# The gather of an mLSTM stage in matmuls of 32 stationary columns, at a higher priority

## The chip, the cores and the metric

The kernel runs on one core of a Trainium2 chip. The metric is the device time of one execution in microseconds (us). The time before is the median of three runs, 572.12 us (571.66 to 572.26). Profiles are taken of one execution.

## The reference

An mLSTM runs over 768 tokens for 4 batches of 8 heads with 40 values a head; its output, 3072 tokens of 320 values, goes through a gated feed-forward network of width 1536.

```
for t in range(S):
    m_new = max(f[t] + m, i[t])
    C = exp(f[t] + m - m_new) * C + exp(i[t] - m_new) * outer(v[t], k[t])
    n = exp(f[t] + m - m_new) * n + exp(i[t] - m_new) * k[t]
    y[t] = sigmoid(o[t]) * (C @ q[t]) / max(abs(n @ q[t]), 1)
x = y.transpose(0, 2, 1, 3).reshape(B * S, H * D)
out = (sigmoid(x @ w_gate) * (x @ w_val)) @ w_out
```

## The kernel before

The recurrence is worked out in chunks of 128 tokens. A unit `u = (c, b)` is chunk `c` (0 to 5) of batch `b` (0 to 3), all 8 heads of it: 24 units. Within a unit the contribution of its own tokens is a matrix product: `dm[u]`, 128 source tokens by 8 heads by 128 target tokens, holds decays times scores, and `vt[u]`, 128 tokens by 8 heads by 41, holds the values with a column of ones, which gives the denominator. What came before the chunk is in the state `cst`.

A unit passes through five stages. `st_a` transposes q and k. `st_b` makes the scores on TensorE, in groups of 3, 3 and 2 heads, and multiplies each group into `dm[u]` on VectorE (L427 in chunks 0 and 1, L435 afterwards). `st_c` does the part with the state (`in`, L447, for chunks after the first), then the gather: for each head one f32 matmul with `dm[u][:, h, :]` as the stationary operand, 128 columns, and `vt[u][:, h, :]`, 41 columns, as the moving one, into `pv` in PSUM (`av`, L452). VectorE adds `pv` to the state's part (L454) and the denominator and output gate follow. `st_d` transposes the result (`xt`, L488) and splits it into a high and a low f32r part. `st_e` updates the state (`cs`, L500).

The feed-forward network runs in between, chunk by chunk: `ffn_up` (L532, L534, L537 into `pg`) and `ffn_down` (L554 to L556 into `po`), each product as three f32r products of high and low parts. Its matmuls move 256, 512 or 320 columns. Weights come from DRAM and are decoded and split on the other engines during the first part of the kernel.

The order is set in two ways. The first two units' work, `opening`, is emitted in an order by hand, with its own `gather` (L697). After it all events (stages of units, tiles of the network, weight parts) are sorted by the positions in `PARAM['pos']` and emitted one after another; a scheduler then orders the instructions of each engine by priority, which falls with the order of emission, as far as dependences allow. `tc.high_priority(offset=n)` lifts the instructions in its block by n places; stages a to d are emitted with an offset of `PARAM['HPO']`, 1. TensorE runs its queue in the resulting order.

PSUM tiles of the stages come from `bank`, two buffers of the tag `pa` in turn. The gate transposes of `gate_transpose` (L195) are small matmuls on 32 partitions.

Of the kernel before, what the change touches and what calls it, by code (L numbers as in the profile page):

```python
# [67 lines left out]
    },  # L68
    'unpin': [],
}  # L70
GROUPS = ((0, 3), (3, 3), (6, 2))

# [2 lines left out]
def mlstm_then_gated_ffn_kernel(  # L75
# [13 lines left out]
    nc = tc.nc  # L89
    B, H, S, D = q.shape  # L90
    P = 128
# [30 lines left out]
    qt, kt, vt, ot = {}, {}, {}, {}  # L122
# [18 lines left out]
    dm = {}  # L141

    def dm_tile(c, b):
        dm[(c, b)] = big.tile([P, H, L], F32, tag="dmat", name=f"d_{c}_{b}", bufs=3)
        return dm[(c, b)]
# [193 lines left out]
    def bank(c, b, shape, name):  # L339
        return ps_a.tile(shape, F32, tag="pa", name=f"{name}_{c}_{b}")  # L340
# [51 lines left out]
    def stack():  # L392
# [6 lines left out]
        for x, dst, i in ((1, ks, 0), (0, qs, 1)):  # L399
# [4 lines left out]
            nc.sync.dma_start(dst[one].rearrange("p (m g) t -> p m (g t)", m=3).bitcast(F32),  # L404
                              sc[:, 0, :, x, :].rearrange("m d w -> d m w"))

    dlast = {}

    def d_last(u):
# [29 lines left out]
    def st_c(c, b):  # L439
        u = (c, b)  # L440
        nc.scalar.activation(ot[u], ot[u], AF.Tanh, scale=0.5)
        t1 = None
        if c > 0:
            pi = bank(c, b, [P, H, DA], "in")
            for g, (h0, nh) in enumerate(GROUPS):
                r = nh * D
                nc.tensor.matmul(pi[:, h0 : h0 + nh, :], qk[u][:r, g, :], cst[:r, b, g, : nh * DA], start=True, stop=True)  # L447
            t1 = two.tile([P, H, DA], F32, tag="t1", name=f"t1_{c}_{b}")
            nc.vector.tensor_tensor(t1, pi, dec[:, c, b * H : (b + 1) * H].unsqueeze(2).broadcast_to([P, H, DA]), ALU.mult)
        pv = bank(c, b, [P, H, DA], "av")  # L450
        for h in range(H):
            nc.tensor.matmul(pv[:, h, :], dm[u][:, h, :], vt[u][:, h, :], start=True, stop=True)  # L452
        if c > 0:
            nc.vector.tensor_tensor(t1, t1, pv, ALU.add)  # L454
            hs = t1
        else:
            hs = pv
        halfden(u, hs)
        times_den(u)
# [4 lines left out]
    def halfden(u, hs):  # L464
        c, b = u
        den = two.tile([P, H], F32, tag="den", name=f"den_{c}_{b}")
        nc.vector.tensor_scalar(den, hs[:, :, D], -2.0, 2.0, ALU.mult, ALU.max)
        nc.vector.scalar_tensor_tensor(den, hs[:, :, D], 2.0, den, ALU.mult, ALU.max)
        nc.vector.reciprocal(den, den)
        rden[u] = den  # L470
        nc.vector.scalar_tensor_tensor(ot[u], ot[u], 1.0, hs[:, :, :D], ALU.add, ALU.mult)

    def times_den(u):
        c, b = u
        xin[u] = x = two.tile([P, 3 * P], F32, tag="x", name=f"x_{c}_{b}", bufs=1)
        eng = E('ro0' if c == 0 and b < 2 else 'ro')
        eng.tensor_tensor(x[:, :DM].rearrange("p (h d) -> p h d", d=D), ot[u],
                          rden[u].unsqueeze(2).broadcast_to([P, H, D]), ALU.mult)
        E('xd0' if c == 0 and b < 2 else 'xd').tensor_copy(x[:, DM:], x[:, 2 * P : DM])
# [94 lines left out]
    def opening():  # L574
        us = ((0, 0), (0, 1))
# [48 lines left out]
        d = [dm_tile(0, b) for b in range(2)]  # L624
# [5 lines left out]
        pmb, pt, ps, pv, pc, px, sp = {}, {}, {}, {}, {}, {}, {}  # L630
# [5 lines left out]
        def ptile(tag, shape, name):  # L636
            return (ps_a if tag == "pa" else ps_o).tile(shape, F32, tag=tag, name=name)
# [56 lines left out]
        def gather(b):  # L694
            pv[b] = p = ptile(tags["v", b], [P, H, DA], f"av_0_{b}")
            for h in range(H):
                nc.tensor.matmul(p[:, h, :], d[b][:, h, :], vt[us[b]][:, h, :], start=True, stop=True)  # L697

        def ogate(b):
            nc.scalar.activation(ot[us[b]], ot[us[b]], AF.Tanh, scale=0.5)  # L700
# [7 lines left out]
        w = {x: None for x in ((0, 0), (1, 0), (2, 0))}  # L708
# [25 lines left out]
        for b in range(2):  # L734
            for n in range(2):
                op(f"sp{b}{n}", spread, (b, n))
                op(f"ex{b}{n}", expd, (b, n), f"sp{b}{n}")
                op(f"mk{b}{n}", mask, (b, n), f"ex{b}{n}")
            op(f"dl{b}", d_last, (us[b],), f"mk{b}0", f"mk{b}1")
            for g in range(3):  # L740
                op(f"tr{b}{g}", trans, (b, g))
                op(f"cp{b}{g}", copy, (b, g), f"tr{b}{g}")
                op(f"qb{b}{g}", qbd, (b, g), f"cp{b}{g}")
                op(f"sc{b}{g}", score, (b, g), f"qb{b}{g}")
                op(f"ti{b}{g}", times, (b, g), f"sc{b}{g}", f"dl{b}")
            op(f"kw{b}", kweight, (b,), f"dl{b}", *(f"tr{b}{g}" for g in range(3)))
            op(f"og{b}", ogate, (b,))
            op(f"ga{b}", gather, (b,), *(f"ti{b}{g}" for g in range(3)))
            op(f"na{b}", norm_a, (b,), f"ga{b}", f"og{b}")
            op(f"nb{b}", norm_b, (b,), f"na{b}")  # L750
            op(f"xt{b}", st_d, us[b], f"nb{b}")
# [33 lines left out]
    start = [0.0]  # L785
# [9 lines left out]
    for u in range(2, NU):  # L795
        for st in "abcde":
            c, b = divmod(u, B)
# [16 lines left out]
    for u in reversed(range(2, NU)):  # L814
# [5 lines left out]
        n = u + (1 if u == B * (PARAM['V32'] + 1) - 1 else 2)  # L820
# [19 lines left out]
    for u in range(2, NU):  # L840
        c, b = divmod(u, B)
# [18 lines left out]
    def emit(p, kind, kk):  # L860
# [7 lines left out]
        elif kind == "w":  # L868
            with tc.high_priority(offset=PARAM["WPO"]):
                w_next(wseq[kk])  # L870
        elif kind == "g":
            if kk == 0:
                dmat_load(1, 0)
            else:
                gates_of(2, NCH)
        elif kind == "h":
            gate_transpose(ag, at, *((1, 2), (2, NCH))[kk], None)
        elif kind == "k":
            gates_turn(*((1, 2), (2, NCH))[kk])
        elif kind == "e":  # L880
            if last is None:
                dmat(c, b)
            else:
                with tc.issue_after(last.ins):
                    dmat(c, b)
        else:
            with tc.high_priority(offset=PARAM["HPO"]):
                if kind == "a":
                    st_a(c, b)
                elif kind == "b":  # L890
                    st_b(c, b)
                elif kind == "c":
                    st_c(c, b)
                    st_e(c, b)
                    prefetch(c + 1, b)
                else:
                    st_d(c, b)
# [45 lines left out]
```

## Time and profile before

| | |
|---|---|
| median of three runs | 572.12 us |
| span of the profiled execution | 569.9 us |
| gathers after the opening (L452) | 22 units, 352 matmul records |
| gathers in the opening (L697) | 2 units, 32 matmul records |
| TensorE matmuls and weight loads | 3587 each |
| granted TensorE clock, mean | 0.988 |

The profile names engines PE (TensorE matmuls), PEld (TensorE weight loads), DVE (VectorE), ACT (ScalarE), POOL (GpSimd). A row of a group has the line, the engine, the operation, output and inputs with shapes, the count, then busy us and mean ns of one, then the idle time of the engine ahead of it and what ended it. A record `128*128` is rows by stationary columns; `128x41` is the moving operand. An f32 matmul shows as two records, an f32r one as one. The records of matmuls overlap, so the distance from one start to the next tells more than a duration. The chain of work that ended last is followed back from the end of the kernel, step by step, to what released each piece.

### The profile page before, as it was taken

How to read it: one execution, taken by the hardware profiler on the slowest of the kernel's cores; microseconds unless marked ns; L12 is line 12 of the kernel's file. 1: busy time of each engine (PE TensorE's matmuls, PEld its weight loads, DVE VectorE, ACT ScalarE, POOL GpSimd, SP SyncE). 2: the span in 40 equal slices, each digit the busy share in tenths (PEclk: the TensorE clock that was granted, in tenths of full speed). 3: DMA queues.
4: the chain of work that ended last, by engine and by line, in shares of the span. 5: the costliest groups of instructions: out<-in, count | busy, mean ns of one | idle time of the engine just before them, and what ended most of it. 6: DMA issues, size and time to landing. Idle time of an engine off the chain costs nothing.

```text
span 569.9 us, 9906 instructions
## 1 busy us (share of the span) xinstructions
PE 546.7 (96%) x3587; PEld 497.0 (87%) x3587; DVE 319.5 (56%) x739; ACT 232.2 (41%) x581; POOL 162.2 (28%) x231
## 2 busy tenths in 40 slices
PE   8667999999999999999999999999999999999997
PEld 7565988788899999998888888888888888999996
DVE  5788878895755645555555544545543545432322
ACT  5285657754443442352243241433342332232322
POOL 5567646575420241311322310332210210000000
PEclk9789999999999999999999999999999999999999
DMA  9797747242674947354666544685644824010000
GB/s 197 193 240 185 202 123 192 93 115 54 169 173 119 183 103 182 100 147 125 167 125 156 132 141 129 149 171 124 140 125 134 206 56 121 4 47 2 24 2 23
DMA packets 131641, 72.27 MB, mean 127 GB/s; under 512 B 103113, under 2 KB 120777, under 8 KB 131593
## 3 DMA queue, kind: packets, MB, share of 16 engines
q1 hardware_dynamic: 130504, 71.39, 50.6%
q8 instruction: 28, 0.46, 0.3%
q10 hardware_dynamic: 1088, 0.26, 0.2%
q14 instruction: 21, 0.16, 0.1%
HBM read 56.95 MB, written 14.68 MB: 126 GB/s over the span
## 4 chain that ended last, share of the span: by engine, by line
PE 85%; DVE 7%; ACT 3%; issue 2%; POOL 2%; POOLq 0%; DVEq 0%; ACTq 0%
PE pg L532 34%; PE po L554 7%; PE po L556 7%; PE po L555 7%; PE av L452 6%; PE pg L534 6%; PE pg L537 6%; PE in L447 2%; PE s L434 2%; PE pt L373 2%; PE xt L488 2%; PE cs L500 2%; PE s L426 1%; DVE dc L264 1%; ACT d L226 1%
## 5 line engine op out<-in xcount | busy, mean ns | idle before, releaser
L539 ACT ACTIVATE sg<-pg 128x256 f32<-128x256 f32 (+1 forms) x103 | 48.3, 469 | 174.3 <-PE pg L537 174.2
L540 DVE SCALAR_TENSOR_TENSOR sg<-sg,pg 128x256 f32<-128x256 f32 (+1 forms) x103 | 53.9, 524 | 113.9 <-ACT sg L539 110.6
L532 PE MATMUL pg<-xh,wl 128*128 128x256 f32 (+1 forms) x412 | 111.1, 342 | 1.2 <-POOL wl L304 1.2
L532 PE MATMUL pg<-xh,wh 128*128 128x256 f32 (+1 forms) x412 | 110.9, 343 | 0.4 <-DVE sg L540 0.4
L532 PE MATMUL pg<-xl,wh 128*128 128x256 f32 (+1 forms) x412 | 108.7, 339 | 0.0
L556 PE MATMUL po<-oh,gl 128*128 128x320 f32 x288 | 93.0, 323 | 0.0
L554 PE MATMUL po<-oh,gh 128*128 128x320 f32 x288 | 92.3, 321 | 0.4 <-ACT gh L543 0.4
L555 PE MATMUL po<-ol,gh 128*128 128x320 f32 x288 | 92.4, 321 | 0.0
L544 DVE TENSOR_TENSOR gl<-sg,gh 128x256 fp32r<-128x256 f32 (+1 forms) x103 | 59.6, 579 | 35.5 <-ACT gh L543 34.9
L532 PEld LDWEIGHTS pg<-xh,wl 128*128 128x128 f32 x412 | 70.9, 191 | 8.5 <-POOL wl L304 1.4
L532 PEld LDWEIGHTS pg<-xh,wh 128*128 128x128 f32 x412 | 70.9, 191 | 5.8 <-DVE sg L540 0.6
L532 PEld LDWEIGHTS pg<-xl,wh 128*128 128x128 f32 x412 | 69.3, 190 | 6.6
L543 ACT ACTIVATE gh<-sg 128x256 fp32r<-128x256 f32 (+1 forms) x103 | 51.7, 502 | 47.7 <-DVE sg L540 47.7
L554 PEld LDWEIGHTS po<-oh,gh 128*128 128x128 f32 x288 | 54.5, 189 | 2.0 <-ACT gh L543 0.6
L555 PEld LDWEIGHTS po<-ol,gh 128*128 128x128 f32 x288 | 54.4, 189 | 1.3
L556 PEld LDWEIGHTS po<-oh,gl 128*128 128x128 f32 x288 | 54.2, 188 | 0.5 <-DVE gl L544 0.2
L534 PE MATMUL pg<-xh,w 128*128 128x256 f32 (+1 forms) x206 | 52.9, 332 | 0.7 <-POOL v L139 0.4
L537 PE MATMUL pg<-xl,w 128*128 128x256 f32 (+1 forms) x206 | 53.1, 331 | 0.0
L452 PEld LDWEIGHTS av<-v,d 128*128 128x128 f32 x352 | 46.8, 191 | 2.2 <-DVE d L427 0.6
L452 PE MATMUL av<-v,d 128*128 128x41 f32 x352 | 45.5, 269 | 0.4 <-DVE d L427 0.3
L508 POOL TENSOR_TENSOR cst<-cst,cdec 120x246 f32<-120x246 f32 (+1 forms) x32 | 16.0, 519 | 98.9 <-PE in L447 98.9
L235 POOL TENSOR_SCALAR_AFFINE_SELECT d<-d 128x1024 f32<-128x1024 f32 x22 | 24.2, 1101 | 50.1 <-ACT d L230 46.0
(128 smaller groups left out, 834.5 us busy)
## 6 DMA issues: line engine op xcount, KB each, us to landing
d<-mscr SPq DMA_DIRECT2D x22, 512.0 KB
ks<-scr SPq DMA_DIRECT2D x16, 360.0 KB
qs<-scr SPq DMA_DIRECT2D x16, 360.0 KB
k<-in_k_dram SPq DMA_DIRECT2D x24, 160.0 KB
v<-in_v_dram SPq DMA_DIRECT2D x24, 160.0 KB
o<-in_o_gate_dram SPq DMA_DIRECT2D x24, 160.0 KB
st_o<-in_moe_w_out_dram SPq DMA_DIRECT2D x12, 320.0 KB
out_dram<-ob SPq DMA_DIRECT2D x24, 160.0 KB
```

Of the source, the lines that this page charges most:

```text
L235: nc.gpsimd.affine_select(out=d, in_=d, pattern=[[0, H], [1, L]], compare_op=ALU.is_ge, fill=0.0, base=0, channel_multiplier=-1)
L452: nc.tensor.matmul(pv[:, h, :], dm[u][:, h, :], vt[u][:, h, :], start=True, stop=True)
L532: nc.tensor.matmul(pg[n], w[n][:, a, fs], x[c][:, a, n0:n1], start=(i + a == 0), stop=False)
L534: nc.tensor.matmul(pg[n], w2[n][:, fs], xh[c][:, 2, n0:n1], start=False, stop=False)
L537: nc.tensor.matmul(pg[n], w2[n][:, fs], xl[c][:, 2, n0:n1], start=False, stop=True)
L539: nc.scalar.activation(sg, pg[0], AF.Tanh, scale=0.5)
L540: nc.vector.scalar_tensor_tensor(sg, sg, 1.0, pg[1], ALU.add, ALU.mult)
L543: last = nc.scalar.activation(gh[u][:, :nt], sg, AF.Copy)
L544: E('gl0' if c == 0 else 'gl').tensor_tensor(gl[u][:, :nt], sg, gh[u][:, :nt].bitcast(F32), ALU.subtract)
L554: nc.tensor.matmul(po[t], g1[:, ts], oh[:, j, :], start=(j == 0), stop=False)
L555: nc.tensor.matmul(po[t], g1[:, ts], ol[:, j, :], start=False, stop=False)
L556: nc.tensor.matmul(po[t], g0[:, ts], oh[:, j, :], start=False, stop=(j == NF - 1))
```

## The change

A helper `by_columns` splits one matmul into n matmuls, each with 128/n of the stationary columns (a part of the target tokens) and the whole moving operand, and writes each to the matching partitions of the output. With n = 4 both gathers, in `st_c` and in the opening, issue four matmuls of 32 stationary columns for each head, one quarter of the tokens after another. In `st_c` the gather is emitted with a priority offset of 20 within the block's offset of 1. The entries `SC` and `SPO` of `PARAM` are not used.

```
+    'AV': 4,
+    'SC': 1,
+    'APO': 20,
+    'SPO': 20,
...
+    def by_columns(dst, lhs, rhs, n):
+        w = P // n
+        for x in range(n):
+            xs = slice(x * w, (x + 1) * w)
+            nc.tensor.matmul(dst[xs], lhs[:, xs], rhs, start=True, stop=True)
...
         pv = bank(c, b, [P, H, DA], "av")
-        for h in range(H):
-            nc.tensor.matmul(pv[:, h, :], dm[u][:, h, :], vt[u][:, h, :], start=True, stop=True)
+        with tc.high_priority(offset=PARAM['APO']):
+            for h in range(H):
+                by_columns(pv[:, h, :], dm[u][:, h, :], vt[u][:, h, :], PARAM['AV'])
...
             for h in range(H):
-                nc.tensor.matmul(p[:, h, :], d[b][:, h, :], vt[us[b]][:, h, :], start=True, stop=True)
+                by_columns(p[:, h, :], d[b][:, h, :], vt[us[b]][:, h, :], PARAM['AV'])
```

## Prediction

> **What bounds the kernel now.** I read first the busy line and the chain of the page, then the windows, then the chain in order of time around one gather.
>
> ```profile
> span 569.9 us, 9906 instructions
> PE 546.7 (96%) x3587; PEld 497.0 (87%) x3587; DVE 319.5 (56%) x739; ACT 232.2 (41%) x581; POOL 162.2 (28%) x231
> ...
> PE 85%; DVE 7%; ACT 3%; issue 2%; POOL 2%; POOLq 0%; DVEq 0%; ACTq 0%
> ...
> PE pg L532 34%; PE po L554 7%; PE po L556 7%; PE po L555 7%; PE av L452 6%; PE pg L534 6%; PE pg L537 6%; PE in L447 2%; PE s L434 2%; PE pt L373 2%; PE xt L488 2%; PE cs L500 2%; PE s L426 1%; DVE dc L264 1%; ACT d L226 1%
> ```
>
> TensorE carries 85% of the chain, and the gather (`av`, L452) is 6% of it, some 34 us. The windows say where TensorE is the limit:
>
> ```profile
> core 0: us, PE busy (x) PEld busy (x) DVE busy (x) ACT busy (x) POOL busy (x), PEclk, DMA share, GB/s
> 12.00:30.00 18.00, 12.90 (x68) 10.91 (x68) 13.01 (x27) 7.63 (x22) 10.06 (x15) 0.73 0.81 209
> 60.00:495.00 435.00, 431.28 (x2788) 388.00 (x2786) 250.24 (x582) 176.07 (x427) 127.24 (x171) 1.00 0.54 135
> ```
>
> Between 60 and 495 us matmuls lack only 3.7 of 435 us, and VectorE, the next engine, has 250. What a gather takes there is added to the end or taken from it one for one. Twenty gathers lie in that stretch, two just before it and two in the opening:
>
> ```profile
> L452 PE MATMUL av<-v,d 128*128 128x41 f32 x352 | 45.5, 269 | 0.4 <-DVE d L427 0.3
> ...
> L697 PE MATMUL av<-v,d 128*128 128x41 f32 x32 | 5.3, 338 | 2.2 <-DVE d L689 2.2
> ```
>
> 352 records are 22 units of 16, and 32 are 2: each of 8 heads is two records (an f32 matmul runs as two loads and two matmuls). One unit in the chain, in order of time (start, length, what):
>
> ```profile
> 169.26 0.63 PE in L447 x6
> 169.89 1.75 PE av L452 x16
> 171.65 0.20 PE pg L532
> 171.84 0.57 PE cs L500 x6
> ```
>
> The gather takes 1.75 us, 0.109 a record. What is that? `cs` has 4 records of 120 stationary columns and 2 of 80, 640 columns in 0.57 us, or 0.89 ns each; the gather loads 16 x 128 = 2048 columns, 0.85 ns each. The moving side is far from it (41 columns against up to 123 in `cs`), so the **weight loads** set the pace. For the moving side I take the f32 scores, which move 384 columns, in the chain of the second chunk:
>
> ```profile
> 77.01 0.65 PE s L426 x2
> ```
>
> Two records in 0.65 us, 0.85 ns a column: 41 columns are 35 ns. Today 16 x 35 ns = 0.56 us of movement lie hidden under 1.75 us of loads.
>
> **The change part by part.** *The split.* Each head becomes four matmuls of 32 stationary columns. The columns loaded stay 2048 a unit, as 64 loads of about 32 x 0.87 = 28 ns. The moving operand passes four times: 64 records of 35 ns, 2.24 us if one follows another, against 0.56. So nothing is removed; the change pays only if column groups work beside each other. No row shows that, so I bound it. One after another: 2.24 us. All four groups at once: 16 x 35 ns = 0.56 us. Two at once: 1.12 us. I take two. The reason is the order: the two records of one f32 matmul use the same group and stand next to each other, so the next group's first load can go beside the second load of this one, but the one after that must wait until its own group's first record has started, and matmuls start in order in every row I read. Saved: 1.75 - 1.12 = 0.63 us a unit.
>
> The Trainium skill (TensorEngine Tiling (Array Packing), section Overview) puts the speedup of four groups of 32 columns at up to 4x; by that estimate a gather would be 0.44 us, and no run here shows it.
>
> *The switch.* The only place where TensorE works on a part of its array is the gate transpose L195, on 32 of 128 rows. Matmuls first, then loads:
>
> ```profile
> 93.24 0.47 PE L532 MATMUL pg<-xh,wh 128*128 128x512 f32 x1
> 93.73 0.43 PE L195 MATMUL ptg<-ident,gin 32*128 32x32 f32 x4
> 94.09 0.49 PE L532 MATMUL pg<-xh,wh 128*128 128x512 f32 x1
> ...
> 93.73 0.32 PEld L195 LDWEIGHTS ptg<-ident,gin 32*128 32x128 f32 x4 [0.32 <-DVE qk L359]
> 94.09 0.19 PEld L532 LDWEIGHTS pg<-xh,wh 128*128 128x128 f32 x1
> ...
> L195 PE MATMUL ptg<-ident,gin x11: 221/223/282, 4.7 to 93.9; 32*128 32x32 f32 x11
> ```
>
> Compare a whole-array stretch:
>
> ```profile
> 462.03 0.19 PEld L554 LDWEIGHTS po<-oh,gh 128*128 128x128 f32 x1
> ...
> 462.18 0.31 PE L554 MATMUL po<-oh,gh 128*128 128x320 f32 x1
> 462.33 0.31 PE L452 MATMUL av<-v,d 128*128 128x41 f32 x2
> 462.47 0.40 PE L555 MATMUL po<-ol,gh 128*128 128x320 f32 x1
> 462.70 0.31 PE L452 MATMUL av<-v,d 128*128 128x41 f32 x2
> ```
>
> Normally a load starts some 0.15 us ahead of its matmul. After the 32-row group the next load starts with its matmul, at 94.09. L195's group ends at 93.73 + 0.43 = 94.16 and one of its matmuls takes 0.22 (the median in its row), so the last one started at 93.94 and 0.15 us passed, of which its own 32 columns explain 0.03: 0.12 us of emptying, and the full load of 0.11 us is then exposed, where a gather today exposes 0.11 - 0.035. Leaving costs 0.12 + 0.035 = 0.16 us, and entering the same 0.12 plus the first small load, 0.15: **0.31 us a unit**. Rows are not columns, so the bounds are 0 and 0.31; I take 0.31, as it is the only row. The page above, section Key Properties, also says that a change of the tiling mode drains TensorE; the row agrees, at 0.12 us.
>
> *The priority.* Some gathers are cut up, as at 462.33: a pair of records between `po` matmuls. There a pair with its `po` takes 462.70 - 462.33 = 0.37 us, a `po` alone 0.15, so a pair costs 0.22, 0.11 a record: the same as in one piece. Closing the gather up is worth nothing by itself. It matters because each piece would now pay the switch: 8 pieces would cost 8 x 0.31 = 2.5 us. With an offset of 20 against 32 matmuls I expect one or two pieces. Pulled forward, the gather can reach the multiplication that feeds it too soon:
>
> ```profile
> L435 DVE TENSOR_TENSOR d<-s,d 128x384 f32<-128x384 f32 (+1 forms) x48 | 24.0, 510 | 18.4 <-PE s L434 17.2
> ```
>
> If TensorE waited for one such multiplication in each of 20 units, that is 20 x 0.51 = 10 us; what it now waits before L452 is 0.4 us in all. I take zero, because six of the eight heads use the first two of the unit's three multiplications, and at 1.12 us for eight they take 0.84 us before the third is needed; behind a waiting gather everything on TensorE would queue. Less than zero is excluded: only 3.7 us of idle time could be filled.
>
> *Instructions.* 24 x 48 = 1152 more records with as many loads on TensorE. Nothing shows how fast its queue issues small ones. The nearest row is L195 above: four records start within 0.21 us, 0.06 to 0.07 each, and 64 at that pace would be 4.0 us. That is the upper end; the lower is that issue stays hidden, which I take, since L195's loads are of 128 columns and explain that pace by themselves. No transfer, no buffer and no other engine's instruction changes; the addition (L454), which waited 23.1 us in all for the gather, starts earlier and is off the chain.
>
> ```profile
> L454 DVE TENSOR_TENSOR t<-t,av 128x328 f32<-128x328 f32 x20 | 9.9, 495 | 23.1 <-PE av L452 23.1
> ```
>
> *Sum.* Per unit -0.63 + 0.31 = -0.32 us. The opening's second gather is on the chain too, and longer (the granted clock of that window is 0.73):
>
> ```profile
> 20.15 3.41 PE av L697 x16
> ```
>
> So I count 24: -7.7 us. The span goes from 569.9 to 562.2. The median of the runs is 572.12, 2.2 over the span: **564.4 us**, 1.3% faster.
>
> **The rivals.**
> *All four groups at once.* 0.56 + 0.31 = 0.87 us a unit, -0.88 x 24 = -21 us: 551.0. For it: loads to different columns touch nothing in common. Against: the order of the two records of one matmul. With no cost of switching it is 543.6.
> *One after another (slower).* If groups share one way in for the moving operand, the gather is bound by 64 x 35 ns: 2.24 + 0.31 - 1.75 = +0.80 us, x 24 = +19 us: 591.3. It decides from the point where fewer than about 1.6 groups work together (2.24 / 1.6 = 1.4 = 1.75 - 0.31). For it: the whole trace has one load and one movement at a time.
> *Loads not under matmuls, or issue bound.* 64 x (28 + 35 ns) = 4.0 us, with the switch +2.56 us a unit, +61 us: 633; the issue end above gives the same. Against: today every load lies under the matmul ahead of it, as the 0.109 us a record shows. The Trainium skill (TensorE: Matmul & The Clock Gate, Part 3: Packing small matmuls) says that loads overlap matmuls in flight only when the row group differs, and all four column groups share their rows. The trace disagrees for the whole array, where loads with the same rows do overlap; for parts no run here shows it.
> *Nothing.* The gain equals the switch (about 1.44 us for the split gather), or the narrow matmuls run as before: 572.
>
> **How the numbers follow.** Two at once 0.34, four at once 0.28, one after another 0.20, loads or issue exposed 0.08, nothing 0.10. Within 0.2% (1.1 us, about what a measurement of this kernel can tell) is 0.08, taken mostly from the last. Faster: 0.62; slower: 0.30. The range leaves out the exposed case and the far end of four at once, and keeps one after another and the 10 us wait for multiplications: 548 to 592. Cases of both signs fill it; the likeliest alone, with a switch of 0 to 0.31 us, is 557 to 566.
>
> **What would show it.** A gather of 64 records closed up, and its length in the chain: 1.4 us is my case, 0.9 the first rival, 2.5 the second, over 4 the third. A gap of 0.1 to 0.15 us before its first load and after its last record shows the switch. Pieces of gather between `pg` or `po` matmuls, or waits of the gather for L435, show the priority wrong. I am wrong if small loads do not overlap at all, or if the order of records does not hold groups back.

## The result, and the profile after

The changed kernel takes 607.1 us (median of four runs, 603.54 to 611.93), the kernel before 571.89 us beside it. The ratio is 1.0632, 95% interval 1.0578 to 1.0686: 6% slower, and above the range of the prediction. The profiled execution, the slowest of the four, has a span of 610.1 us, against 569.9 before. Where an execution, here or below, is over 1.5% slower than the fastest of the same kernel at a lower granted clock, it is left out of the comparison.

The page of the changed kernel, the lines that answer to those of before (lines of code stand about eleven further down now: the gather's matmul is L415, in the helper, `pg` is L543 to L548, `po` L565 to L567):

```profile
span 610.1 us, 12187 instructions
...
PE 582.1 (95%) x4739; PEld 498.3 (82%) x4739; DVE 319.9 (52%) x739; ACT 232.4 (38%) x581; POOL 160.9 (26%) x231
...
PEclk9678999999999999999979999969999999999999
...
L415 PE MATMUL av<-v,d 128*32 128x41 f32 x1536 | 50.9, 209 | 2.9 <-DVE d L700 2.8
```

TensorE is busy 35.4 us longer (582.1 against 546.7), and the span is 40.2 us longer. The 1152 additional records are there (4739 - 3587). The gather's own row shows nothing of the loss: 50.9 us, against 45.5 + 5.3 before. Durations in such rows overlap and do not add up to time on the path; the distance from one start to the next has to be read. The timeline of TensorE's matmuls at the fourth gather, which is in one piece (start, length, what):

```profile
59.78 0.40 PE L543 MATMUL pg<-xh,wh 128*128 128x256 f32 x2
60.11 0.82 PE L415 MATMUL av<-v,d 128*32 128x41 f32 x64
60.86 0.38 PE L543 MATMUL pg<-xh,wl 128*128 128x256 f32 x1
...
85.17 0.57 PE L415 MATMUL av<-v,d 128*32 128x41 f32 x36
85.67 0.41 PE L567 MATMUL po<-oh,gl 128*128 128x320 f32 x1
86.01 0.26 PE L415 MATMUL av<-v,d 128*32 128x41 f32 x2
86.20 0.41 PE L565 MATMUL po<-oh,gh 128*128 128x320 f32 x1
86.54 0.26 PE L415 MATMUL av<-v,d 128*32 128x41 f32 x2
```

The 64 records at 60.11 take 60.86 - 60.11 = 0.75 us, where 16 whole ones took 1.75. So the split itself works, better than predicted. The next gather, at 85.17, looks different: 36 records (18 matmuls) stand together, and from there each matmul of the gather, two records, is followed by one of the network, fourteen times. What follows it starts 9.43 us after its own start. Counted over TensorE's order of instructions, the 24 gathers lie in **145 pieces**, and their spans, with the network's matmuls between the pieces, add up to 97.2 us; before there were 65 pieces and 50.7 us.

A lone piece with its `po` takes 86.54 - 86.01 = 0.53 us. A `po` alone takes 0.15, by the rows shown in the prediction. Over the 20 such pieces at full clock the medians are 0.535 and 0.147 us, so the piece costs **0.39 us**, where a whole-array pair cost 0.22. The weight loads of the same stretch say why:

```profile
86.01 0.14 PEld L415 LDWEIGHTS av<-v,d 128*32 128x32 f32 x2 [0.15 <-issue]
86.20 0.19 PEld L565 LDWEIGHTS po<-oh,gh 128*128 128x128 f32 x1
86.54 0.14 PEld L415 LDWEIGHTS av<-v,d 128*32 128x32 f32 x2 [0.15 <-issue]
```

Each load starts at the instant that its matmul's record starts (86.01, 86.20, 86.54), not 0.15 us ahead of it as between whole-array matmuls. The array is emptied on the way into the piece and on the way out, and both first loads lie open. The Trainium skill (TensorEngine Tiling (Array Packing), section Key Properties) says that a change of the tiling mode drains TensorE; the trace agrees here for columns, as it did for rows in the prediction, with 0.15 us in which no load runs ahead of each piece. 145 - 24 = 121 additional pieces at 0.39 us are an estimated 47 us.

### The profile page after: what moved, and what is told of

Same layout as the page of the kernel before. It is cut to its first block, busy times and chain, and to the rows that moved or that the text cites. A ratio compares the mean times of both kernels' runs of the same rounds, so it can differ in the third digit from the quotient of the medians.

```text
span 610.1 us, 12187 instructions
## 1 busy us (share of the span) xinstructions
PE 582.1 (95%) x4739; PEld 498.3 (82%) x4739; DVE 319.9 (52%) x739; ACT 232.4 (38%) x581; POOL 160.9 (26%) x231
## 4 chain that ended last, share of the span: by engine, by line
PE 82%; ACT 5%; POOL 4%; DVE 3%; issue 2%; DMA 1%; SPq 0%; POOLq 0%; DVEq 0%; ACTq 0%
PE pg L543 32%; PE po L565 7%; PE po L566 7%; PE po L567 6%; PE av L415 6%; PE pg L548 6%; PE pg L545 6%; PE in L457 3%; PE cs L511 2%; PE s L444 2%; ACT d L230 2%; PE pt L377 2%; PE s L436 1%; PE xt L499 1%; PE mb L654 1%
## 5 line engine op out<-in xcount | busy, mean ns | idle before, releaser
L543 PE MATMUL pg<-xh,wh 128*128 128x256 f32 (+1 forms) x412 | 112.3, 348 | 3.0 <-ACT sg L550 2.6
L543 PE MATMUL pg<-xh,wl 128*128 128x256 f32 (+1 forms) x412 | 112.5, 346 | 0.0
L543 PE MATMUL pg<-xl,wh 128*128 128x256 f32 (+1 forms) x412 | 111.1, 344 | 0.0
L565 PE MATMUL po<-oh,gh 128*128 128x320 f32 x288 | 94.2, 327 | 0.8 <-ACT gh L554 0.8
L566 PE MATMUL po<-ol,gh 128*128 128x320 f32 x288 | 94.1, 327 | 0.0
L567 PE MATMUL po<-oh,gl 128*128 128x320 f32 x288 | 93.6, 326 | 0.4 <-DVE gl L555 0.4
L555 DVE TENSOR_TENSOR gl<-sg,gh 128x256 fp32r<-128x256 f32 (+1 forms) x103 | 62.0, 602 | 37.3 <-ACT gh L554 36.8
L543 PEld LDWEIGHTS pg<-xh,wh 128*128 128x128 f32 x412 | 72.0, 195 | 10.8 <-ACT sg L550 3.6
L543 PEld LDWEIGHTS pg<-xh,wl 128*128 128x128 f32 x412 | 71.2, 193 | 7.6
L543 PEld LDWEIGHTS pg<-xl,wh 128*128 128x128 f32 x412 | 70.3, 192 | 7.7
L565 PEld LDWEIGHTS po<-oh,gh 128*128 128x128 f32 x288 | 55.0, 191 | 4.3 <-ACT gh L554 1.8
L545 PE MATMUL pg<-xh,w 128*128 128x256 f32 (+1 forms) x206 | 55.7, 338 | 1.1 <-POOL w L312 0.6
L567 PEld LDWEIGHTS po<-oh,gl 128*128 128x128 f32 x288 | 54.9, 191 | 1.8 <-DVE gl L555 0.7
L548 PE MATMUL pg<-xl,w 128*128 128x256 f32 (+1 forms) x206 | 55.2, 337 | 0.0
L415 PEld LDWEIGHTS av<-v,d 128*32 128x32 f32 x1536 | 32.2, 112 | 27.9 <-issue 16.6
L415 PE MATMUL av<-v,d 128*32 128x41 f32 x1536 | 50.9, 209 | 2.9 <-DVE d L700 2.8
L239 POOL TENSOR_SCALAR_AFFINE_SELECT d<-d 128x1024 f32<-128x1024 f32 x22 | 27.3, 1239 | 64.5 <-ACT d L234 56.3
L523 ACT ACTIVATE ct<-cs,rmask 120x82 f32<-120x82 f32 (+1 forms) x80 | 18.8, 314 | 55.3 <-PE cs L511 55.3
```

The source lines that it names most:

```text
L239: nc.gpsimd.affine_select(out=d, in_=d, pattern=[[0, H], [1, L]], compare_op=ALU.is_ge, fill=0.0, base=0, channel_multiplier=-1)
L415: nc.tensor.matmul(dst[xs], lhs[:, xs], rhs, start=True, stop=True)
L543: nc.tensor.matmul(pg[n], w[n][:, a, fs], x[c][:, a, n0:n1], start=(i + a == 0), stop=False)
L545: nc.tensor.matmul(pg[n], w2[n][:, fs], xh[c][:, 2, n0:n1], start=False, stop=False)
L548: nc.tensor.matmul(pg[n], w2[n][:, fs], xl[c][:, 2, n0:n1], start=False, stop=True)
L555: E('gl0' if c == 0 else 'gl').tensor_tensor(gl[u][:, :nt], sg, gh[u][:, :nt].bitcast(F32), ALU.subtract)
```

## The experiments

Two theories stood at first. Theory A: the pieces are the loss, and in one piece the split gains. Theory C: the higher priority is the loss, since it puts the gather ahead of other work. Later texts add theories under further letters and say there what they are.

### The gather closed up, and cut up further

An offset of 40, more than the 32 matmuls of a gather, keeps each gather together (24 pieces); one of 1 cuts most of them apart (332 pieces).

```
-    'APO': 20,
+    'APO': 40,      e1_closed_up
+    'APO': 1,       e2_offset_1
```

> The changed kernel with the offset of the gather's priority at 40 in place of 20: in TensorE's order each of the 24 gathers then stands in one piece (24 pieces in all, against 145 in the changed kernel). Theory A (the cut pieces cost the time: each lone piece of one split matmul costs about 0.39 us, and a closed gather takes 0.75 us with some 0.25 us of switching): 1.0 us a gather against 1.75, times 22 to 24, so 553 to 557 us. Theory B (narrow matmuls are slow in themselves, closed up or not, or the clock falls because only a part of the array works): 590 us or more. Theory C (the higher priority makes TensorE wait for the multiplications that feed the gather): 572 to 585 us, with waits for L445 of several us in all.

> The changed kernel with the offset of the gather's priority at 1: 332 pieces in TensorE's order, 187 more than in the changed kernel. Theory A at 0.39 to 0.45 us a piece: 607 + 73 to 84 = 680 to 691 us. Theory B (narrow matmuls slow in themselves): the same 607 us within 5. Theory C (the priority costs): faster than 607 us.

Closed up: 572.95 us, ratio 1.0016 (0.9991 to 1.0041). Cut up: 690.4 us (a second execution took 704.03). With 24, 145 and 332 pieces the kernel takes 573, 607 and 690 us, so the time follows the pieces. From 24 to 332 it is 0.38 us a piece, of which the lower clock (0.949 against a mean of 0.973) can account for at most 0.05. The bookkeeping of the closed version:

```profile
span 569.0 us, 12196 instructions
...
PE 531.8 (93%) x4739; PEld 472.3 (83%) x4739; DVE 324.8 (57%) x739; ACT 230.9 (41%) x581; POOL 159.5 (28%) x231
```

The changed kernel's TensorE is busy 582.1 - 531.8 = 50.3 us longer than this one: 0.42 us for each of 121 pieces, near the 0.39 read from the timeline. The clock is no rival for this loss: over all executions it is 0.976 on the average in the changed kernel and 0.973 in the closed version, which is 34 us faster. Of the two profiled executions the changed kernel's has 13.7 us more at half clock behind the opening, which can be at most 6.9 of the 50.3 us; without them a piece costs 0.36 us. Theory A holds for the loss. But of the 22 gathers behind the opening 20 took 0.75 us here, and yet the gain over the kernel before, which theory A put at 15 us or more, did not come. (The time lies in theory C's range, but TensorE waits for L445 only 1.8 us in all, and the gather not at all.) TensorE is busy 14.9 us less than before and idle 14.0 us more (569.0 - 531.8 = 37.2, against 569.9 - 546.7 = 23.2).

### Priority alone, and two groups

```
-    'AV': 4,
+    'AV': 1,        e3_priority_alone (APO 20)
+    'AV': 2,        e4_two_groups (APO 40)
```

> The changed kernel with whole matmuls again (one of 128 stationary columns for each head) at the offset of 20: the priority alone, 24 pieces. Theories A and B: 570 to 573 us, as before the change, because a cut in whole matmuls costs nothing. Theory C: 576 us or more.

> Two matmuls of 64 stationary columns for each head, offset 40, 24 pieces. Theory A with groups side by side: 32 records, two at a time; a load of 64 columns is about 56 ns, so 16 times 56 ns = 0.9 us, with the switch 1.15 us a gather against 1.75: 557 to 562 us, behind the four groups. Theory B: between 572 and 607 us.

Priority alone: 575.86 us, ratio 1.0062 (1.0031 to 1.0092). The same offset of 20 that cuts 32 matmuls leaves 8 in one piece (24 pieces in all), and that costs about 4 us: theory C has a little of the truth, at most about a tenth of the loss. Two groups: 576.19 us, ratio 1.0061 (1.003 to 1.0093), with gathers of 1.06 us, close to what was expected of them, while the time was not. Among these three early places (offsets of 20, 40 and 40) a gather shorter by 0.7 us a unit changes nothing, and one shorter by 1 us brings 3 us.

### The gather in its own place, in one piece

All matmuls of a gather get one priority, and the count goes on afterwards as if there had been 8 (in the opening only the count is set so):

```
-        with tc.high_priority(offset=PARAM['APO']):
-            for h in range(H):
-                by_columns(...)
+        p0 = tc.cur_priority
+        for h in range(H):
+            tc.cur_priority = p0 - PARAM['APO']
+            by_columns(...)
+        tc.cur_priority = p0 + H
```

With `APO` 1 (36 pieces) the gather stands where the kernel before had it; with 12 (24 pieces) it is ahead of a part of the state's matmuls `in`, in 12 of 20 units.

> The split gather with the scheduler's counter held: all 32 matmuls of a gather carry one priority (that of its first matmul less 1), and the counter goes on after 8 places as before the change, so that the rest of the program is shifted less. 36 pieces; the gather stays behind the stage's other work, where it was before the change. Theory D (in the closed-up run the shorter gather did save its 0.75 us, and what took it back is the other order of the rest, above all the gather pulled far ahead): 24 times 0.75 us saved, 12 more pieces at 0.39 us: 555 to 564 us. Theory E (the stretch is not bound by TensorE as tightly as it looks, and any shorter gather ends in waits for other engines): 569 to 574 us.

> As the run before, but with the one priority of the gather 12 places ahead: 24 pieces, the gather pulled ahead of the state's matmuls (in, L457). Theory D: slower than the run before although it has fewer pieces, 560 to 572 us. Theory E: 569 to 574 us, the same as the run before. If only pieces counted: 5 us faster than the run before.

In place: **565.11 us**, ratio 0.9877 (0.9837 to 0.9916), faster than both kernels, just outside theory D's 555 to 564 us and clear of theory E's. Ahead: 568.16 us, 0.9937 (0.9914 to 0.9959), as theory D has it. The version with fewer pieces is the slower one, so beside the pieces the place matters. The timeline in place:

```profile
58.84 0.82 PE L415 MATMUL av<-v,d 128*32 128x41 f32 x64
59.58 0.42 PE L569 MATMUL po<-oh,gl 128*128 128x320 f32 x1
59.84 0.30 PE L567 MATMUL po<-oh,gh 128*128 128x320 f32 x1
59.98 0.31 PE L568 MATMUL po<-ol,gh 128*128 128x320 f32 x1
```

The first `po` after the gather takes 0.26 us to the next start, the second 0.14: leaving costs 0.12 us here. For entering, the changed kernel's row at 59.78 shows two `pg` in 0.33 us to the gather's start, where one takes 0.12 (59.49 to 59.61 below): 0.09 us. A closed gather costs 0.09 + 0.75 + 0.12 = 0.96 us.

The controls are the same place with whole arrays and with two groups:

> The same place for the gather as in the version of 565.1 us (all its matmuls at one priority, one place ahead of the rest of its stage), but each head one matmul of 128 columns (AV 1). Theory D (the gain of that version comes from the shorter gather; where the gather stands is worth nothing): about 572 us, and a closed gather of 1.75 us. Theory G (the gain comes from the place, the split adds little): 565 to 568 us.

> The same place, each head two matmuls of 64 columns (AV 2), gathers of about 1.06 us, as in the other run with two groups. Theory D: between whole and four, in proportion to the time of a gather (1.75, 1.06, 0.75 us): 567 to 570 us. Theory G: the same as with four, 565 to 566 us.

Whole: 573.3 us, ratio 1.0019 (0.9989 to 1.0049), 26 pieces, near theory D. Two groups: 566.95 us, 0.9905 (0.9875 to 0.9934), 28 pieces, at the lower edge of theory D. So the gain is the split's and not the place's, and closing a whole-array gather up is worth nothing, as predicted. Two groups and four cannot be told apart in time: their intervals overlap. A whole gather in place:

```profile
57.47 1.87 PE L415 MATMUL av<-v,d 128*128 128x41 f32 x16
59.17 0.48 PE L545 MATMUL pg<-xh,wh 128*128 128x256 f32 x2
59.49 0.28 PE L545 MATMUL pg<-xh,wl 128*128 128x256 f32 x1
59.61 0.73 PE L513 MATMUL cs<-v,k 128*120 128x123 f32 x6
```

It takes 1.70 us, and the two `pg` behind it 0.32 in place of 0.24: leaving costs 0.08 us here too, so that a whole gather costs 1.78 us against 0.96. The three pages, whole, two and four:

```profile
span 572.8 us, 9911 instructions
...
PE 548.0 (96%) x3587; PEld 497.0 (87%) x3587; DVE 317.6 (55%) x739; ACT 232.2 (41%) x581; POOL 160.8 (28%) x231
```

```profile
span 565.3 us, 10680 instructions
...
PE 536.0 (95%) x3971; PEld 478.7 (85%) x3971; DVE 323.9 (57%) x739; ACT 232.1 (41%) x581; POOL 158.2 (28%) x231
```

```profile
span 563.2 us, 12202 instructions
...
PE 532.4 (95%) x4739; PEld 474.5 (84%) x4739; DVE 324.9 (58%) x739; ACT 232.4 (41%) x581; POOL 157.5 (28%) x231
```

| in place | TensorE busy | idle (span less busy) | span |
|---|---|---|---|
| whole | 548.0 | 24.8 | 572.8 |
| two groups | 536.0 | 29.3 | 565.3 |
| four groups | 532.4 | 30.8 | 563.2 |

From whole to four, 24 gathers at 0.82 us less are 19.7 us, less 10 additional pieces at 0.39: 15.8 us, and 15.6 were measured. Of these, 6.0 us came back as idle time and 9.6 reached the span: 62%. These are single executions; by the medians (573.3 and 565.11) 8.2 us reached the time, 52%.

### Half the gather

Here the kernel before runs one whole-array matmul for each pair of heads, 82 moving columns wide, so it leaves out the gather of every even head behind the opening; the priority count goes on as for two.

```
-        for h in range(H):
-            nc.tensor.matmul(pv[:, h, :], dm[u][:, h, :], vt[u][:, h, :], ...)
+        for h in range(0, H, 2):
+            nc.tensor.matmul(pv[:, h : h + 2, :], dm[u][:, h + 1, :], vt[u][:, h : h + 2, :], ...)
+            tc.cur_priority += 1
```

> The kernel before with half of the gather: one whole matmul for each pair of heads, with the odd head's decays for both and 82 moving columns, so 8 records of 0.11 us in place of 16; the gather of every even head is left out. No column groups, no switch. It asks whether TensorE time saved in the gather comes back one for one. Theory D (TensorE is the bound): 0.87 us a unit less, times 20 to 22: 553 to 557 us. Theory E: 566 to 573 us.

559.31 us, ratio 0.9776 (0.9746 to 0.9806):

```profile
span 557.8 us, 9550 instructions
...
PE 528.3 (95%) x3411; PEld 475.6 (85%) x3411; DVE 326.0 (58%) x739; ACT 232.3 (42%) x581; POOL 161.0 (29%) x231
```

With no split and no new place, TensorE is busy 18.4 us less (528.3 against 546.7) and the span is 12.1 us shorter (557.8 against 569.9): 66% is returned (68% by the medians), about as in the version in place, and between the two expectations. So time taken from the gather isn't returned one for one in this kernel, in either of two ways of taking it away.

### One group after the other

The closed version with the column group as the outer loop, so that eight matmuls of one group follow each other:

```
+            w = P // PARAM['AV']
+            for x in range(PARAM['AV']):
+                xs = slice(x * w, (x + 1) * w)
+                for h in range(H):
+                    nc.tensor.matmul(pv[xs, h, :], dm[u][:, h, xs], vt[u][:, h, :], ...)
```

> The closed-up gather with its loops exchanged: all 8 heads of one column group after another, then the next group, so that 16 records in a row use the same 32 columns. If the speed of the split gather comes from four groups at work at once: 64 records at 35 ns, 2.2 to 2.4 us a gather in place of 0.75, so 573 + 22 times 1.55 = 605 to 610 us. If it comes from small loads alone: the same 0.75 us and 570 to 576 us.

591.64 us, ratio 1.0339 (1.0295 to 1.0384), 13 us below what was expected of groups that work at once: TensorE is busy 29.4 us longer than in the closed version (561.2 against 531.8), as the longer gathers would have it, but idle 8.7 us less. The timeline of its matmuls:

```profile
57.46 2.23 PE L466 MATMUL av<-v,d 128*32 128x41 f32 x64
59.63 0.41 PE L570 MATMUL po<-oh,gl 128*128 128x320 f32 x1
```

The same 64 records take 59.63 - 57.46 = 2.17 us: 34 ns each, the movement of 41 columns, one after another. With the groups in turn they take 0.75 us. The short time comes from groups working beside each other; small loads alone do not bring it.

### Where the closed version lost its gain

In the closed version the chain at 325 us showed GpSimd's copy for the transposes (L490, `x<-x`) behind the next unit's subtraction (L233), which waited for a DMA; in the kernel before the copy came first. If such waits ate the gain, moving the copy to VectorE should give some of it back. The control is the kernel before with the same move.

```
-  'xd0': 'v',
+  'xd0': 'v', 'xd': 'v',
```

> The gather with an offset of 40, in four groups (572.95 us), and the small copy of x for the transposes (L490) on VectorE instead of GpSimd, so that it no longer stands behind the next unit's subtraction that waits for its DMA. Theory D (the closed gather's gain was lost in such waits of other engines' orders): the wait of xt for that copy goes, at some 2 us in each of the units where it was seen, and the time falls by 2 to 8 us, to 565 to 571 us. Theory H (the lost gain lies elsewhere): 572 to 574 us.

> The control of that run: the kernel before with the same copy on VectorE and nothing else changed. There the copy stands ahead of the subtraction already, so both theories expect 571 to 573 us; a fall as large as in the closed version would say that the copy's place has nothing to do with the split.

Closed: 575.74 us, ratio 1.0077 (1.0046 to 1.0109). Before: 575.59 us, 1.0079 (1.0047 to 1.011). Each is slower than the same version without the move, by 2.8 and 3.7 us, and neither expectation was met. The waits of TensorE in the closed version (who waits for whom: us in total, times, longest):

```profile
PE xt L499 <- POOL x L488: 4.8, 2, 3.7
PE ptg L199 <- ACT cst L523: 4.0, 1, 4.0
PE cs L511 <- DVE t L459: 2.9, 1, 2.9
PE s L436 <- DVE d L437: 2.6, 3, 1.2
PE xt L499 <- POOL x L490: 2.0, 1, 2.0
```

And with the copy on VectorE:

```profile
PE xt L499 <- POOL x L488: 4.8, 2, 3.7
PE pt L361 <- DVE at L201: 3.9, 2, 3.1
PE xt L499 <- DVE cst L528: 3.2, 2, 1.6
PE cs L511 <- DVE t L459: 2.9, 1, 2.9
```

The wait for L490, which occurred once, is gone, and waits for other work of VectorE (L201, L528) are there in its place; TensorE's idle time is 573.4 - 533.4 = 40.0 us, against 37.2. The explanation by this one copy falls. That the lost gain sits in waits of TensorE is measured (14.0 us more idle than before); which order of the other engines brings it about was not settled.

## Why the prediction was wrong

**The pieces: the step that failed.** The prediction said "each piece would now pay the switch: 8 pieces would cost 8 x 0.31 = 2.5 us. With an offset of 20 against 32 matmuls I expect one or two pieces." The price was near (0.39 us measured). The count was not: six pieces to a gather on the average, up to 17. An offset of 20 closes 8 matmuls up (24 pieces in the run with priority alone), one of 40 closes 32 up (24 pieces), and 20 does not close 32 up (145). The likely mechanism: the matmuls of a gather follow each other by one place of priority, so those beyond the offset rank among the network's matmuls, and the two sequences alternate. The runs with an offset of 1 bear it out, with 332 pieces where the count runs on and 36 where all 32 matmuls have one priority, though there the count behind the gather was changed too. 121 pieces at 0.39 us are 47 us, and TensorE's busy time against the closed version gave 50.3; the closed version being busy 14.9 us less than the kernel before, 47 - 14.9 = 32 of the 35.4 us that TensorE is busy longer are accounted for. The prediction named pieces between `pg` and `po` as a sign of being wrong, but gave them no rival and no chance, so its range left the case out.

**Two groups at once.** It took 1.12 us on the ground that the two records of one f32 matmul hold the next group back. They don't: 0.75 us with four groups, 1.06 with two, 2.17 with one. That is the first rival's mechanism, and its figure of 0.56 us too: in the middle of a closed gather four records pass in 36 ns, 0.58 us for all 64, and the rest of the 0.75 lies at the ends. The Trainium skill (TensorE: Matmul & The Clock Gate, Part 3: Packing small matmuls), by which loads overlap matmuls in flight only when the row group differs, does not agree with these traces: all four groups share their rows, and 64 loads and 64 movements fit into 0.75 us, where the movements alone take 2.17 us in one group.

**The switch.** Taken as 0.31 us from a 32-row matmul. Around a closed gather it is 0.09 + 0.12 us and the 0.17 us at the gather's own ends, 0.38 in all; a lone piece costs 0.39, of which 0.02 is its own share of the 0.58. So the price is much the same for a lone piece and for a whole gather, a fifth above what was taken. That it stands at both ends was right, but a whole gather pays 0.08 us on leaving as well.

**Waits and issue.** No wait of the gather for the scores' multiplication appears: of the 2.9 us in its row 2.8 are the opening's (L700). Issue of small instructions stayed hidden, at 12 ns a record in the closed gather. Both were costed at nothing, rightly.

**One for one.** "What a gather takes there is added to the end or taken from it one for one" failed as well, and hid behind the pieces. Of time taken from TensorE 52 to 62% (in place) and 66 to 68% (half the gather) reached the end; the rest turned into idle time of TensorE. The argument had been that matmuls lacked only 3.7 us of 435 between 60 and 495 us. That says what limits the kernel as it stands, not how far behind the next limit is: between the fourth gather and the last, matmuls lack 3.7 us before, 5.4 in place with whole arrays, 9.0 in place with four groups and 14.4 closed up with an offset of 40.

The predicted 564.4 us is near the version in place (565.11) by luck, by two errors that cancel: the split gives more than was taken, and less of it comes through. (The 557 to 566 us that it gives for its likeliest case are 557.0 to 564.4 by its own terms.)

## What to carry to other kernels

A matmul that uses a part of TensorE's columns should be emitted so that its whole set stays in one piece, with one priority for all of it; the number of pieces in TensorE's order is to be counted before the gain is. Here two groups in turn gained most of what four did (6.4 of 8.2 us). A saving on an engine busy for 96% of the span should be discounted for the waits that come up under it, here by a third to a half, and in the version with an offset of 40, where the work is also moved ahead of its place, by all of it.

## What the hardware showed beyond that

In one closed gather four matmul records, one from each group, start about 7, 7, 6 and 16 ns apart, and four groups pass in about 36 ns, which is one movement of 41 columns (34 ns a record with one group alone). Behind the last record 0.13 us pass to the next matmul's start.

The granted clock fell in two of the cut stretches. The windows of the changed kernel:

```profile
300.00:400.00 100.00, 99.83 (x762) 81.14 (x748) 48.72 (x105) 31.70 (x71) 21.83 (x34) 0.94 0.56 133
400.00:495.00 95.00, 94.85 (x661) 78.10 (x662) 43.34 (x100) 32.03 (x68) 19.47 (x24) 0.95 0.55 132
```

Behind 0.94 and 0.95 are two stretches of 10.24 us at half clock, from 303.6 and 399.2 us, each beginning inside a gather cut into 13 pieces (299.7 to 309.6 and 395.2 to 405.1). Three gathers in 15 to 17 pieces had no such stretch. In the kernel before and in the version in place the clock of this part is 1.00. The trace of the run in 332 pieces has eight such stretches between 60 and 629 us, 85 us together, and each begins inside a gather in 16 pieces or more; six other such gathers had none. The five traces with whole arrays (the kernel before, the priority alone, in place and whole, half the gather, and the kernel before with the copy on VectorE) have none there. So cutting and half clock go together. It is not the cutting alone: the closed version, with each gather in one piece, also had two such stretches, of 3.4 us. What brings the clock down was not tried by itself.
